# A batched two-stage attention with a squared-relu MLP: batch 0 cut by head sets and token parts, one PSUM tile with fixed banks, a new written order

## The chip, the cores and the metric

The kernel runs on one core of one Trainium2 chip. The metric is the device time of one execution in microseconds (us). Five engines work side by side, each in the order of its own instructions: PE (matrix products, with weight loads that overlap them), DVE and ACT (element-wise work; both can read PSUM, where PE puts its results), POOL and SP (here they issue DMA transfers, POOL the loads that turn float32 into bfloat16, SP the stores and the crossbar transposes).

## What is computed

```python
def _attn_ref(q, k, v, p):            # q, k, v: (8, 8, 576, 64); p: (8, 8, 32, 64)
    p_packed = sm_attn(p, k, v)       # softmax(p k^T / 8) v : 32 packed rows a head
    return sm_attn(q, p_packed, p_packed)

x = attn_out.transpose(0, 2, 1, 3).reshape(4608, 512)
h = x @ w_in                          # 512 x 2048
g = s * relu(h) ** 2 + b
out = g @ w_out                       # 2048 x 512
```

## The kernel before

**Stages.** Everything is done batch by batch (576 tokens each). A batch's q, k and v are loaded as 96 rows (`R`) by head by six tokens' columns; `Tk`/`Tq` (function `on_pe`) turn k and q on PE for batches 0 and 1, `Dk`/`Dq` (`on_dma`) by crossbar transposes from SP for batches 2 to 7. Heads are taken in two sets, a = 0 (even heads) and a = 1 (odd ones), and in four groups g. `F b.a` is the first attention's scores of one set and their exp; `P b` the packed rows and their division; `X b` turns them; `S b` is the second attention's scores and exp; `A b.a` the sums by a product with a block matrix of ones, then ln and exp(-x) on ACT and one multiplication on DVE, which gives the weights `aT`. The packed rows are multiplied into `w_in` first (`W b.ch`, chunks of 512 columns, result `pw`), so the first layer is `M b.m`: four products of 288 columns of `aT` with `pw`, 16 blocks m a batch, a relu on ACT (now and then DVE) and a square on DVE into `gT`. `O b.t x n` does n of the 16 products of one output tile; the last of them is followed by one scaling step on DVE (`ysb`) and by stores. The constant `b` comes in through `BT`/`BC`: sums of `w_out`'s columns by small products, then a float32 product with `rowsf` that adds four partial rows, into `biasrep`.

**Order.** A long written list of such words is run from top to bottom, and every instruction stays in that order on its engine (`keep_in_program_order`). A word issues its products and also the ACT and DVE steps that belong to them at that point. Loads stand in POOL's order, transposes and stores in SP's. What a word reads and what still occupies its buffer are its waits. `Z n` and `Y n` are n products of zeros of 512 columns, which only keep PE going; 12 more stand ahead of the list.

**Batch 0** differs: loads of k, q, v come in two halves by heads, its second scores and weights run by halves of the tokens (`weights_half`, `weigh_half`, `h 0.m.hf`), for two m blocks of the first layer in that form and for twelve in the usual one.

**Buffers.** PSUM has two pools: `psh` (two pairs of banks, for scores, W pairs, M) and `psy` (four single banks, for output tiles, packed rows, idle products). `rawp` has one buffer each for raw k, q and v; so the next load of k waits until its transposes have been read. `kT`, `qT` have two; `gT` holds three batches; `ysb` has five.

Of the kernel before, what the change touches and what calls it, by code (L numbers as in the profile page):

```python
# [14 lines left out]
def kernel(  # L15
# [32 lines left out]
    JJ = NP // 16  # L48

# [8 lines left out]
    psh = ctx.enter_context(tc.tile_pool(name="psh", bufs=2, space=bass.MemoryType.PSUM))  # L58
    psy = ctx.enter_context(tc.tile_pool(name="psy", bufs=4, space=bass.MemoryType.PSUM))
# [17 lines left out]
    early = []  # L77

    def big(dt=F32):
        if early:  # L80
            return early.pop()
        return psh.tile([P, 2, NB if dt == F32 else 2 * NB], dt, tag="h", name="hps")
# [12 lines left out]
    pn = [constp.tile([P, 2, 2, D], BF16, name=f"pn{i}") for i in range(2)]  # L95
    pall = constp.tile([16 * (B - 2), 16, 2, D], BF16, name="pall")
# [10 lines left out]
    rowsf = constp.tile([P, P], F32, name="rowsf")  # L107
# [7 lines left out]
    def load(what, b, h0=0, h1=H):  # L115
        src = {"k": k, "q": q, "v": v}[what]
        if h0 == 0:
            raw[what, b] = rawp.tile([R, H, NC * D], BF16, tag=what + "n", name=what + "n")
        pool.dma_start(
            out=raw[what, b][:, h0:h1, :],  # L120
            in_=src[b, h0:h1].rearrange("h (r c) d -> r h (c d)", c=NC),
        )

# [21 lines left out]
    def load_sb():  # L145
        sp.dma_start(out=svec[:], in_=moe_s[0:1].unsqueeze(0).to_broadcast([P, 1]))
        sp.dma_start(out=bvec[:], in_=moe_b[0:1].unsqueeze(0).to_broadcast([P, 1]))
# [6 lines left out]

    def prep_p(b):
        pt = big(BF16)
        for x in range(2):
            tr(
                pt[:, 0, x * P:(x + 1) * P],
                pn[b][:, x, :, :],  # L160
                identb[:],
            )
        for c2 in range(2):
            act.copy(
                out=pbd[D * c2:D * c2 + D, :, b, :, c2, :],
                in_=pt[D * c2:D * c2 + D, 0, 0:2 * P].rearrange("p (g a j) -> p a g j", g=4, a=2),
            )

    def prep_pall():
        n = 16 * (B - 2)  # L170
        pts = [psy.tile([P, 8 * P], BF16, tag="y", name="pps") for _ in range(2)]
# [6 lines left out]
        for x in range(2):  # L178
            src = pts[x][:].rearrange("p (t n) -> p t n", n=P)[:, :, 0:n].rearrange(
# [9 lines left out]
    def on_pe(b, what, half):  # L189
        dst = (kT if what == "k" else qT)[b % 2]  # L190
        if what == "q":
            dst = dst[:].rearrange("p h c r -> p (h c r)")
        tpw = big(BF16)
        tp = [tpw[:, 0], tpw[:, 1]]
        split = b == 0 and what == "q"
        if split:
            tp[1] = psy.tile([P, 2 * NB], BF16, tag="y", name="tps")
        for h4 in range(4):
            for cp in range(CP):
                o = (h4 % 2) * HS + cp * R  # L200
                tr(
                    tp[h4 // 2][:, o:o + R],
                    raw[what, b][:, 4 * half + h4, cp * P:(cp + 1) * P],
                    identb[0:R, 0:R],
                )
        d = dst[:, half * 4 * HS:(half + 1) * 4 * HS].rearrange("p (a s) -> p a s", a=2)
        if split:
            act.copy(out=d[:, 0], in_=tp[0][:, 0:2 * HS])
            vec.tensor_copy(out=d[:, 1], in_=tp[1][:, 0:2 * HS])
        else:  # L210
            vec.tensor_copy(out=d, in_=tpw[:, :, 0:2 * HS])
# [8 lines left out]
    def order_v(b, h0=0, h1=H):  # L220
        vec.tensor_copy(
            out=vr[:, :, h0:h1, 0:D].rearrange("r c h d -> r h c d"),
            in_=raw["v", b][:, h0:h1, :].rearrange("r h (c d) -> r h c d", c=NC),
        )

    def first_scores(b, a):
        if a == 0:
            e1[b] = attp.tile([R, 2, NC, 4, NP], BF16, tag="e1", name="e1")
        s1 = big()
        for g in range(4):  # L230
            for cp in range(CP):
# [8 lines left out]
                )  # L240
        act.activation(
# [8 lines left out]
    def packed(b, half=None):  # L250

        if not half:
            pps[b] = psy.tile([P, NB], F32, tag="y", name="pps")
        pp = pps[b][:, 0:2 * DV].rearrange("p (a x) -> p a x", a=2)
        for a in range(2):
            for c in range(NC):
                for g in range(4) if half is None else (2 * half, 2 * half + 1):
# [8 lines left out]
        if half == 0:  # L266
            return
        rd = smp.tile([P, 2], F32, tag="rd", name="rd")
        vec.reciprocal(out=rd[:], in_=pp[:, :, D])
        pk[b] = smp.tile([P, 2, 2, D], BF16, tag="pk", name="pk")  # L270
        for a in range(2):
# [6 lines left out]
    def turned(b):  # L278

        pt = pps[b][:, NB // 2:].bitcast(BF16)  # L280
        for a in range(2):
            tr(pt[:, a * P:(a + 1) * P], pk[b][:, a].rearrange("p c d -> p (c d)"), identb[:])
        vec.tensor_copy(
            out=ppd[b % 2][:].rearrange("p a g j -> p (a g j)"),
            in_=pt[:, 0:2 * P],
        )

    def second_scores(b, by_half=False, with_w=False):
        e2[b] = attp.tile([P, 2, S], BF16, tag="e2", name="e2")
        tiles = [big() for _ in range(2)]  # L290
        for a in range(2):
            for g in range(4):
                for c2 in range(2):
                    t, i = (c2, a) if by_half else (a, c2)
                    mm(
                        tiles[t][NP * g:NP * g + NP, i, 0:HS],
# [6 lines left out]
        if by_half:  # L303
            exp_half(b, tiles, 0, 0)
            exp_half(b, tiles, 1, 0)
            s2[b] = tiles
            return
        if with_w:
            packed_w(b, [0])
        for a in range(2):  # L310
            act.activation(
# [6 lines left out]
    def exp_half(b, tiles, a, hf):  # L318
        act.activation(
            out=e2[b][:, a, hf * HS:(hf + 1) * HS],  # L320
            in_=tiles[hf][:, a, 0:HS],
            func=AF.Exp,
            scale=scale,
        )

    def weights_half(b, hf):
        if hf == 0:
            aT[b] = atp.tile([P, 2, S], BF16, tag="aT", name="aT")
        dps = big()
        for a in range(2):  # L330
            mm(dps[:, a, 0:HS], onesbd[:], e2[b][:, a, hf * HS:(hf + 1) * HS], start=True, stop=True)
        if hf == 0:
            exp_half(b, s2[b], 0, 1)
            exp_half(b, s2[b], 1, 1)
        ld = smp.tile([P, 2, HS], F32, tag="ld", name="ld")
        act.activation(out=ld[:], in_=dps[:, :, 0:HS], func=AF.Ln)
        rcd[hf] = smp.tile([P, 2, HS], F32, tag="rcd", name="rcd")
        act.activation(out=rcd[hf][:], in_=ld[:], func=AF.Exp, scale=-1.0)

    def weigh_half(b, hf):  # L340
        cols = slice(hf * HS, (hf + 1) * HS)
        vec.tensor_tensor(out=aT[b][:, :, cols], in0=e2[b][:, :, cols], in1=rcd[hf][:], op=ALU.mult)

    def weights(b, a):
        if a == 0:
            aT[b] = atp.tile([P, 2, S], BF16, tag="aT", name="aT")
        dps = big()
        for hf in range(2):
            mm(dps[:, hf, 0:HS], onesbd[:], e2[b][:, a, hf * HS:(hf + 1) * HS], start=True, stop=True)
        ld = smp.tile([P, 2, HS], F32, tag="ld", name="ld")  # L350
        act.activation(out=ld[:], in_=dps[:, :, 0:HS], func=AF.Ln)
        rc = smp.tile([P, S], F32, tag="rcd", name="rcd")
        act.activation(out=rc[:], in_=ld[:].rearrange("p a s -> p (a s)"), func=AF.Exp, scale=-1.0)
        vec.tensor_tensor(out=aT[b][:, a, :], in0=e2[b][:, a, :], in1=rc[:], op=ALU.mult)

    def packed_w(b, chs):
        if b not in pw:
            pw[b] = atp.tile([P, 2, DFF], BF16, tag="pw", name="pw")
        where = {}
        if len(chs) > 1:  # L360
            pair = [big() for _ in range(2)]
            where = {(a, x): pair[a][:, x, :] for a in range(2) for x in range(2)}
        if len(chs) != 2:
            single = [psy.tile([P, NB], F32, tag="y", name="wps") for _ in range(2)]
            where.update({(a, len(chs) - 1): single[a][:] for a in range(2)})
        for x, ch in enumerate(chs):
            for g in range(4):
                for a in range(2):
                    mm(
                        where[a, x][NP * g:NP * g + NP],  # L370
                        ppd[b % 2][D * a:D * a + D, a, g, :],
                        w_in_sb[D * a:D * a + D, g, ch * NB:(ch + 1) * NB],
                        start=True,
                        stop=True,
                        tile_position=(D * a, NP * g),
                    )
        if len(chs) > 1:
            for a in range(2):
                dst = pw[b][:, a, chs[0] * NB:(chs[0] + 2) * NB].rearrange("p (i f) -> p i f", f=NB)
                evict(dst, pair[a][:], a == 0)  # L380
        if len(chs) != 2:
            ch = chs[-1]
            if b == 0 and ch == 0:
                s2["w"] = single
                first_w(b, 0)
                return
            for a in range(2):
                evict(pw[b][:, a, ch * NB:(ch + 1) * NB], single[a][:], a == 0)

    def first_w(b, half):  # L390

# [329 lines left out]
```

The softmax here doesn't subtract the row's maximum and nothing guards it: scores larger than these inputs give would overflow.

## Time and profile before

| What | us |
|---|---|
| three runs | 250.62, 251.31, 251.28 (median 251.28) |
| span of the profiled execution, first to last instruction | 248.0 |
| the same execution's total | not listed |
| PE busy / DVE busy / ACT busy | 241.6 / 144.4 / 140.6 |
| first product / end of the last product | 1.19 / 244.59 |

Stages by the timeline: batch 0's first layer starts at 20.37; batch 1's first scores at 36.69, batch 2's at 67.05; the second scores of batch 2 at 75.53. The last DVE step starts at 244.63 and the last store follows it.

```profile
DMA  6999999999696589939798999337998811121133
GB/s 74 174 206 208 201 203 204 197 204 162 136 213 140 140 138 144 225 89 193 115 209 169 160 147 226 85 80 156 146 230 133 185 37 50 42 46 42 42 87 86
```

These two rows of the page cut the span into 40 slices of 6.2 us: the busy share of the DMA engines in tenths, and the GB/s that they moved. In a table of groups, columns are line, engine, operation, output<-inputs, shape and count, then busy us and mean ns of one, then idle time just before and what ended it. Nearly everything has line L62, L65 or L73, since helpers record the instructions; one reads by the names of tiles. `hps` is a pair of banks of `psh`, `yps` an output tile, `zps` (and `hps<-zb`) the idle products.

### The profile page before, as it was taken

How to read it: one execution, taken by the hardware profiler on the slowest of the kernel's cores; microseconds unless marked ns; L12 is line 12 of the kernel's file. 1: busy time of each engine (PE TensorE's matmuls, PEld its weight loads, DVE VectorE, ACT ScalarE, POOL GpSimd, SP SyncE). 2: the span in 40 equal slices, each digit the busy share in tenths (PEclk: the TensorE clock that was granted, in tenths of full speed). 3: DMA queues.
4: the chain of work that ended last, by engine and by line, in shares of the span. 5: the costliest groups of instructions: out<-in, count | busy, mean ns of one | idle time of the engine just before them, and what ended most of it. 6: DMA issues, size and time to landing. Idle time of an engine off the chain costs nothing.

```text
span 248.0 us, 5518 instructions
## 1 busy us (share of the span) xinstructions
PE 241.6 (97%) x2302; PEld 134.2 (54%) x2302; DVE 144.4 (58%) x278; ACT 140.6 (57%) x218; POOL 29.1 (12%) x43
## 2 busy tenths in 40 slices
PE   8999899999999999999999999999999999999994
PEld 2655565356644665456544654466545654366453
DVE  4438875599564864386538753586348742767221
ACT  2266742558837772758555953888266844578000
POOL 8733212000300012000300030000200000000000
PEclk9999999999999999999999999999999999999999
DMA  6999999999696589939798999337998811121133
GB/s 74 174 206 208 201 203 204 197 204 162 136 213 140 140 138 144 225 89 193 115 209 169 160 147 226 85 80 156 146 230 133 185 37 50 42 46 42 42 87 86
DMA packets 59450, 35.50 MB, mean 143 GB/s; under 512 B 32160, under 2 KB 54944, under 8 KB 59424
## 3 DMA queue, kind: packets, MB, share of 16 engines
q0 software_dynamic: 25184, 18.61, 50.8%
q1 hardware_dynamic: 34192, 16.49, 30.2%
q8 instruction: 18, 0.29, 0.5%
q14 instruction: 8, 0.07, 0.1%
q10 hardware_dynamic: 48, 0.03, 0.0%
HBM read 37.23 MB, written 9.44 MB: 188 GB/s over the span
## 4 chain that ended last, share of the span: by engine, by line
PE 82%; DMA 16%; issue 1%; POOL 0%; DVE 0%; POOLq 0%
PE yps L62 49%; PE hps L62 31%; DMA w_out_sb<-in_moe_w_out_dram 14%; DMA kn<-in_k_dram 2%; PE pps L62 1%; PE pps L65 1%; POOL kn L73 0%; DVE ysb L73 0%; POOL identb L73 0%; POOLq L73 0%; POOLq L705 0%
## 5 line engine op out<-in xcount | busy, mean ns | idle before, releaser
L62 PE MATMUL yps<-w_out_sb,gT 128*128 128x512 bf16 (+1 forms) x592 | 147.8, 374 | 0.6 <-DMA w_out_sb<-in_moe_w_out_dram 0.6
L73 ACT ACTIVATE rlu<-hps 128x576 bf16<-128x576 f32 x124 | 77.0, 649 | 23.1 <-PE hps L62 19.9
L62 PEld LDWEIGHTS <-gT 128*128 128x128 bf16 x592 | 54.8, 98 | 50.9 <-issue 8.8
L62 PE MATMUL hps<-aT,pw 128*128 128x288 bf16 x512 | 78.3, 285 | 0.2 <-ACT rlu L73 0.2
L73 DVE TENSOR_TENSOR gT<-rlu 128x576 bf16<-128x576 bf16 x128 | 57.8, 457 | 26.1 <-ACT rlu L73 23.3
L62 PEld LDWEIGHTS <-pw 128*128 128x128 bf16 x512 | 49.7, 97 | 26.3 <-issue 1.2
L73 DVE SCALAR_TENSOR_TENSOR ysb<-yps,svec,biasrep 128x512 f32<-128x512 f32 (+1 forms) x37 | 27.0, 733 | 21.7 <-PE yps L62 21.5
L73 ACT ACTIVATE e<-hps 96x768 bf16<-96x768 f32 (+2 forms) x34 | 21.8, 693 | 30.8 <-PE hps L62 30.6
L73 ACT CAST pw<-hps 128x1024 bf16<-128x1024 f32 x14 | 14.2, 1012 | 21.6 <-PE hps L62 21.0
L73 DVE TENSOR_TENSOR aT<-e,rcd 128x576 bf16<-128x576 bf16 x16 | 12.1, 757 | 23.4 <-ACT rcd L73 23.2
L73 POOL DMA_DIRECT2D kn<-in_k_dram x9 | 6.9, 767 | 130.1 <-DMA kT<-kn 97.8
L73 DVE CAST pw<-hps 128x1024 bf16<-128x1024 f32 x14 | 17.1, 1220 | 4.7 <-PE hps L62 4.6
L62 PE MATMUL zps<-zb 128*128 128x512 bf16 x42 | 13.6, 452 | 1.2 <-DVE zb L73 1.2
L73 ACT ACTIVATE rcd<-ld 128x576 f32<-128x576 f32 x16 | 10.9, 683 | 0.5
L73 ACT ACTIVATE ld<-hps 128x576 f32<-128x576 f32 x16 | 10.3, 643 | 1.2 <-PE hps L62 0.4
L62 PEld LDWEIGHTS <-ppd 64*32 64x32 bf16 x384 | 3.8, 88 | 11.0 <-issue 8.1
L62 PEld LDWEIGHTS <-zb 128*128 128x128 bf16 x56 | 5.6, 108 | 7.2 <-issue 3.2
L73 DVE RECIPROCAL rd<-pps 128x2 f32<-128x2 f32 x8 | 1.4, 171 | 13.3 <-PE pps L62 13.3
L62 PE MATMUL hps<-w_in_sb,ppd 64*32 64x512 bf16 x224 | 8.9, 381 | 0.0
L62 PEld LDWEIGHTS <-kT 128*128 128x128 bf16 x192 | 6.9, 98 | 2.5 <-issue 0.5
L73 DVE COPY vr<-vn 96x3072 bf16<-96x3072 bf16 (+1 forms) x9 | 8.0, 893 | 0.1
L73 POOL DMA_DIRECT2D vn<-in_v_dram x9 | 6.7, 751 | 5.5 <-DVE vr L73 2.9
(58 smaller groups left out, 104.0 us busy)
## 6 DMA issues: line engine op xcount, KB each, us to landing
out_dram<-ysb SPq DMA_DIRECT2D x23, 192.0 KB, 2.6
kn<-in_k_dram POOLq DMA_DIRECT2D x7, 576.0 KB, 7.1
vn<-in_v_dram POOLq DMA_DIRECT2D x7, 576.0 KB, 10.7
qn<-in_q_dram POOLq DMA_DIRECT2D x7, 576.0 KB, 13.3
out_dram<-ysb SPq DMA_DIRECT2D x24, 128.0 KB, 2.4
w_in_sb<-in_moe_w_in_dram POOLq DMA_DIRECT2D x4, 512.0 KB, 14.3
w_out_sb<-in_moe_w_out_dram POOLq DMA_DIRECT2D x4, 512.0 KB, 18.7
out_dram<-ysb SPq DMA_DIRECT2D x23, 64.0 KB, 2.1
```

The lines of the kernel that those rows point to most:

```text
L62: return tc.keep_in_program_order(nc.tensor.matmul(*a, **kw))
L65: return tc.keep_in_program_order(nc.tensor.transpose(*a, **kw))
L73: return lambda *a, **kw: tc.keep_in_program_order(f(*a, **kw))
```

## The change

Batch 0 is cut anew. k and v come in two parts by head set (even heads, then odd), q in two parts by tokens (`PARTS`: four of each row's six tokens, then two); p comes from SP in float32 and DVE doubles and converts it. F, P, X and V of batch 0 run set by set; second scores (`S 0.u.a`), exp (`e`), sums (`d`), ln (`l`), exp(-x) (`i`) and multiplication (`G`) are words of their own for each part u and set a; its W runs in eight chunks of 256 columns, and its whole first layer in words `h 0.m.u` of two m blocks and one part.

The pools `psh` and `psy` are replaced by one tile of eight banks; each word names its banks (`@2`, `@6,2`). Functions become generators: a word's first mention issues its products, each later mention the next step on ACT or DVE, with a letter for the engine where there is a choice. An output tile's scaling and stores are the word `Q`. W of the other batches is issued chunk by chunk. The sum of the four partial bias rows moves from PE to DVE. `w_in` comes in parts in another order, with batch 1's k, v and q ahead of most of `w_out`; the scalars s and b come late, from POOL. The written order is new throughout; the idle products are 12 ahead of it and 26 in it, where there were 12 and 44.

```diff
+    PARTS = ((0, 2), (2, 3))
...
-    psh = ctx.enter_context(tc.tile_pool(name="psh", bufs=2, space=bass.MemoryType.PSUM))
-    psy = ctx.enter_context(tc.tile_pool(name="psy", bufs=4, space=bass.MemoryType.PSUM))
+    psp = ctx.enter_context(tc.tile_pool(name="psp", bufs=1, space=bass.MemoryType.PSUM))
...
+    banks = psp.tile([P, 8, NB], F32, name="banks")
+    spots = []
+
+    def take(n, dt=F32):
+
+        x = spots.pop(0)
+        t = banks[:, x:x + n, :]
+        return t if dt == F32 else t.bitcast(dt)
...
         pool.dma_start(
-            out=raw[what, b][:, h0:h1, :],
-            in_=src[b, h0:h1].rearrange("h (r c) d -> r h (c d)", c=NC),
-        )
+            out=raw[what, 0][:, 4 * part:4 * part + 4, :],
+            in_={"k": k, "v": v}[what][0].rearrange("(g a) (r c) d -> a r g (c d)", a=2, c=NC)[part],
+        )
+
+    def load_p0():
+        sp.dma_start(out=p0f[:], in_=p[0].rearrange("(x g) j d -> (g j) x d", x=2))
...
+    def scores0(u, a):
+        cols, w = part(u)
...
+        if u not in s2:
+            s2[u] = take(2)
+        qh = qT[0][:].rearrange("p h c r -> p h (c r)")
+        for g in range(4):
+            for c2 in range(2):
+                mm(
+                    s2[u][NP * g:NP * g + NP, c2, a * w:(a + 1) * w],
+                    ppd[0][D * c2:D * c2 + D, a, g, :],
+                    qh[D * c2:D * c2 + D, head(a, g), cols],
...
+    def inverse0(u, a):
+        act.activation(out=rcd["r", u][:, a], in_=rcd["l", u][:, a], func=AF.Exp, scale=-1.0)
...
-        ps = big()
-        mm(ps[:, 0, :], rowsf[:], biasrep[:], start=True, stop=True)
-        vec.tensor_scalar_mul(out=biasrep[:], in0=ps[:, 0, :], scalar1=bvec[:])
+        yield
+        vec.tensor_copy(out=bias4[:], in_=ps[0:NP, 0, :])
+        for g in range(1, 4):
+            vec.tensor_tensor(out=bias4[:], in0=bias4[:], in1=ps[NP * g:NP * g + NP, 0, :], op=ALU.add)
+        for g in range(4):
+            vec.tensor_scalar_mul(out=biasrep[NP * g:NP * g + NP], in0=bias4[:], scalar1=bvec[0:NP])
...
-        Lwi0 Lwi1 Lwo0 Lwi2 Lwi3 Lwo1 Lp1 Tk0.0 Z10 PD Tk0.1 Lk1 PP0 Z3 F0.0 V0.0 F0.1 Z5 P0.0 V0.1 Lv1
-        P0.1 Z1 Tq0.0 Z1 X0 Z1 Tq0.1 Lq1 Lwo2 Lwo3 Lpall Z3 S0 Z3 A0.0 Z1 W0.0 A0.1 G0.0 E Y8 h0.0.0
...
+        Lq0.1 Lp1 Lwi2.4 Z4@6 Tk0.0@2 Tk0.0a PD0 PP0@1 Lwi1.2 PP0v PP0a Z2@0 Tk0.1@4 Tk0.1v V0.0 Tk0.0a
+        Tk0.1a F0.0@6 F0.1@0 Lwi0.1 F0.0 Z2@3 P0.0@2 P0.0 Z3@6 X0.0 X0.0v F0.1 V0.1 Z3@0 P0.1 Z1@0
+        Tq0.0@4 Lk1 P0.1 X0.1 Z1@0 Tq0.1@3 Tq0.0a S0.0.0@6 X0.1a Tq0.0v S0.0.1 e0.1 Tq0.1v Z1@2 S0.1.0@0
+        Tq0.1a e0.0 Z2@2 S0.1.1 e1.0 d0.1@4 l0.1 d0.0 l0.0 Z1@6 W0.3@2 e1.1 i0.0 W0.3v PD1 W0.3v W0.2@6
+        d1.1@4 l1.1 i0.1 W0.2v W0.2a G0.0 i1.1 d1.0 l1.0 PP1@0 Lwi6.8 Lv1 G0.1 W0.1@2 W0.1v PP1a PP1v
+        Z2@1 h0.6.0@6 W0.1v i1.0 G1.0 h0.4.0@4 W0.0@0 h0.6.0a Lwi4.6 G1.1 h0.4.1@2 h0.6.0 h0.2.0@6
...
+        h0.10.1a Lpall Tq1.0v Tq1.1v h0.14.0 h0.8.0v h0.8.0 S1@6,2 S1 O0.1x2@4 PA O0.1x2 A1.0@6 S1
+        O0.0x1@5 A1.0 O0.3x1@0 h0.8.1 W1.3@2 W1.3a W1.3v O0.2x1@1 A1.1@6 A1.1 A1.1 O0.3x2 PPA0@2,3
...
+        O0.2x2 BT@2 O0.1x1 O0.0x1 Lk2 M1.0@6 M1.0a O0.1x1 PPA0 PPA0 O0.0x1 Lsb O0.3x1 Lv2 O0.3x1 M1.10
+        O0.1x1 O0.3x1 M1.6@6 O0.3x1 PPA0 BT O0.2x3 M1.6a M1.0 O0.0x1 M1.7@2 O0.0x2 Lq2 M1.7v M1.14@6
+        M1.14a V2 O0.0x2 M1.7 M1.6 M1.1@2 M1.1a M1.3@6 Dk2 O0.2x1 O0.0x2 O0.1x1 Lv3 O0.1x1 M1.9@2 M1.9a
+        O0.3x2 M1.1 O0.0x3 M1.3v M1.3 O0.2x1 F2.0@6 Dq2 O0.0x2 M1.9 PPA0 F2.0 Q0.3 M1.14 F2.1@2 F2.1
+        Q0.0 O0.2x2 M1.4@6 M1.4a P2.1@0 P2.1 M1.2@2 M1.15@6 X2 O0.1x2 M1.2a X2v M1.15a O0.1x1 Q0.1 M1.15
+        S2@2,6 S2 O1.0x1@0 S2 M1.4 M1.2 O0.2x2 M1.8@4 A2.0@2 A2.0 O0.2x2 A2.1@6 A2.1 M1.8v M1.8 O0.2x1
...
```

## The prediction

> **What bounds the kernel now.** I read the page first, then the groups of instructions by form, the busy times of three stretches, the timeline at the seams between stages, and last the landing times of the loads.
>
> ```profile
> span 248.0 us, 5518 instructions
> PE 241.6 (97%) x2302; PEld 134.2 (54%) x2302; DVE 144.4 (58%) x278; ACT 140.6 (57%) x218; POOL 29.1 (12%) x43
> PE 82%; DMA 16%; issue 1%; POOL 0%; DVE 0%; POOLq 0%
> ```
>
> ```profile
> L62 PE MATMUL zps<-zb 128*128 128x512 bf16 x42 | 13.6, 452 | 1.2 <-DVE zb L73 1.2
> L62 PE MATMUL hps<-zb 128*128 128x512 bf16 x14 | 3.7, 379 | 0.0
> L62 PE MATMUL hps<-biasrep,rowsf 128*128 128x512 f32 x2 | 1.1, 630 | 0.1
> ```
>
> ```profile
> 0.00:20.37 20.37, 18.92 (x200) 9.79 (x201) 9.76 (x30) 8.37 (x15) 12.04 (x21) 1.00 1.07 156
> 20.37:55.00 34.63, 33.11 (x356) 18.05 (x355) 25.43 (x47) 18.30 (x30) 5.58 (x7) 1.00 1.31 205
> 55.00:244.59 189.59, 189.59 (x1749) 106.37 (x1746) 108.74 (x203) 113.91 (x175) 11.47 (x15) 1.00 0.71 132
> ```
>
> ```profile
> 1.19 5.30 PE L62 MATMUL zps<-zb 128*128 128x512 bf16 x12 [1.19 <-DVE zb L73]
> 7.23 2.32 PE L62 MATMUL zps<-zb 128*128 128x512 bf16 x10
> 20.37 0.65 PE L62 MATMUL hps<-aT,pw 128*128 128x288 bf16 x4
> 60.05 0.65 PE L62 MATMUL hps<-aT,pw 128*128 128x288 bf16 x4
> 60.54 0.38 PE L62 MATMUL yps<-w_out_sb,gT 128*128 128x512 bf16 x1
> 72.13 1.47 PE L62 MATMUL yps<-w_out_sb,gT 128*128 128x512 bf16 x6
> 73.53 0.67 PE L62 MATMUL hps<-w_in_sb,ppd 64*32 64x512 bf16 x16
> 74.13 1.47 PE L62 MATMUL yps<-w_out_sb,gT 128*128 128x512 bf16 x6
> ```
>
> In the windows the columns are the stretch, then busy time (and count) of PE, weight load, DVE, ACT and POOL, clock, DMA share and GB/s. From 55 us to the last product PE has no gap at all. Its "97%" also counts 56 products of zeros, which do nothing. So the right question is how much of PE's time goes to products that are needed. I take starts, since durations overlap: an output product costs 0.2157 us (92 of them and the half ones run from 227.99 to 244.59), four first-layer products 0.49 (60.05 to 60.54). The same reading elsewhere gives 12 transposes 0.51, 12 first-score products 0.35, a chunk pair of W about 0.46, S 0.28, a sum pair A 0.245. A stretch on small array tiles costs extra at each edge: 72.13 to 73.53 is 1.40 where six products need 1.294, and the way back costs as much; start-to-start gaps give 93 and 95 ns. With these prices on the written order, the needed work is 223.6 us (70 edges among it, 6.6). The rest up to 244.59: start 1.19, idle products 14.6 (12 at 0.427 and 44 at 0.2157), waits 5.2. By 20.37, the first product of batch 0's first layer, only 4.9 us of needed work is done, so 15.5 us are lost there; 5.5 more are lost by 55 (8 idle products, 1.7, and 3.8 of waits).
>
> **What the Trainium skill says.** *TensorE: Matmul & The Clock Gate*, Part 1, has PE start at half clock until it has been busy for some 3.4 us; the trace agrees in size (0.427 against 0.216 us a product before and after about 7.2 us), though the clock column shows full speed. *TensorEngine Tiling (Array Packing)*, Key Properties, says a change of tiling mode drains the engine; the 93 and 95 ns are that price here. *DMA: Bandwidth & Descriptors*, Queues, rings and completion order, says each DMA engine goes round robin over its queues by packet, so a crossbar transpose beside a load slows both; the trace before never overlaps the two, so it cannot confirm this.
>
> **The change, part by part.** *Idle products.* 56 become 38: 12+4 at the head and 22 more. 18 at the warm price are 3.9 us of PE time; that is time only where something needed is ready instead.
>
> *Bias.* Two float32 products (0.93 us from 47.47 to 48.40) go. On DVE one 0.68 and one 0.75 become one copy, three adds from PSUM (as ysb, 0.75) and four multiplies (0.3 to 0.75; I take 0.4): 4.5 us, 3.0 more. DVE is then four us behind by my running sum, and M1.7 needs the bank those adds read; output products stand there on PE. Bounds 0 and 1.5; I take 0.5.
>
> *Batch 0's chain up to the first first-layer product.* k by head sets lands as now (5.86 and 8.23), p comes by SP earlier, off the path. The four extra idle products at the head end at 7.6 (two at half clock), so Tk0.0 starts then instead of at 6.29. ACT has four copies (0.64, 0.37, 0.64, 0.64, overlapping by about 0.06) to 10.1, and F0.0 reads 32 columns of the next heads, which lie in the other set, so both sets must be there: 10.3 (11.01 now). Exp 0.80, P0.0 at 11.75, its divisions, X0.0 at 12.95, then V0.1 on DVE (0.7), P0.1 at 14.25, Tq0.0 to 15.4, its 768-column copy on ACT (0.8) to 16.0, S0.0.1 at 16.45. The exps start at 16.75, as now (16.73): the head start is spent in the queues of ACT and DVE. ACT then holds eleven steps of 384 or 192 columns in a row (pitch about 0.43 and 0.26) until i0.1 ends at 20.6; G0.1 (0.55) ends at 21.3 and h0.6.0 starts at 21.35, one us later than now. But it has done more: W0.3, W0.2, W0.1 and PP1 are in, 5.96 us of needed work against 4.90. Nothing is won or lost here. Later arrivals of q by its 512 and 256 byte runs would add; bounds -1 and +1.
>
> *From there to the end.* Needed work is 223.6 - 0.9 - 5.96 = 216.75 (edges are again 70: W is split in four, but put beside other small-tile work). One more idle group of 4 is 0.86. PE so ends at 21.35 + 216.75 + 0.86 + W = 238.96 + W against 244.59, W being all waits after h0.6.0. The gain is 5.6 - W, so everything hangs on W (now 3.8 and 1.7 of idle products).
>
> W, first part: between h0.6.0 and S1 PE has 14.15 us of work, ACT 13.8 by its pitches, DVE 16.1. DVE starts 0.85 late (first product, relu), so it ends 2.8 behind; the last 1.6 us of it (h0.8.0 and h0.14.0) hold nobody up, and queue gaps cost about 0.8: 2.0, bounds 0.5 and 4. The loads in that stretch fit: the same bytes at the same rate put k1 at 22.7, w_in's rest at 25.2 and 30.6, q1 at 33.5, w_out from 36 to 44.4, each just ahead of its first use in the order.
>
> W, second part: batch 2's first stage is drawn forward, F2.0 from 67 to 54 and S2 from 75.5 to 58.9 plus earlier waits. It needs k2 and q2 loaded and turned.
>
> ```profile
> 40.89 0.77 POOL L73 DMA_DIRECT2D qn<-in_q_dram  x1 [1.36 <-PE pps L65]
> DMA to landing us min/median/max: 13.5/13.5/13.5
> L73 SPq DMA_TRANSPOSE qT<-qn x6: 2531/2840/3331, 56.3 to 189.2; - x6
> DMA to landing us min/median/max: 4.8/6.0/6.5
> ```
>
> q2 lands at 54.3 now, and the bytes ahead of it are the same. Its transpose takes 6.0 us: 60.5 at best, beside S2 at 58.9 + 2.5 = 61.4: no wait. At worst k2's transpose (from 48.7, beside the loads of v2 and q2) shares the engines fully: two back to back take 8.4 us (issued 56.30, landed 64.72), so one adds 4.2 and q2 lands at 58.5; then v3, queued as soon as V2 is done, adds its 2.9 to Dq2: 67.4, a wait of 6. Half of the 4.2 and none of the 2.9 gives 62.4, 1.0 late; between that and no wait I take 0.5. On SP the stores Q0.3 and on stand behind Dq2; five ysb buffers cover that.
>
> W, third part: from 60 us on ACT and DVE are never more than 2.9 us behind PE by the same sum, with three pairs of banks for first-layer products where there were two; 0.5 (0 to 2). Store order, Lsb on POOL, v0 by sets and the single pool with fixed banks cost nothing beside this: POOL is busy 12% of the span, and banks are waited for just as pool buffers were.
>
> W = 2.0 + 0.5 + 0.5 + 0.5 = 3.5. PE ends at 242.5. After it now come 3.4 us of store; Q7.1, a whole tile, now ends only 0.8 us before the last half tile, +0.2. Span 246.1. Around the span lie 251.28 - 248.0 = 3.3 us (the profiled execution's own total is not listed; I use the median of 250.62, 251.31, 251.28): **249.4 us**.
>
> **Rivals.** *B, hardly any wait (W = 1.3):* DVE's surplus hides behind squares nobody needs, and transposes overlap loads, as read and write side differ. For it: the uses stand just behind the landings. Against it: ACT, DVE and PE are all full at once. 247.2. *C, slower:* the transposes of batch 2 share the DMA engines with loads. PE is in order, so it stands at S2 although w_out and gT for dozens of output products are there. With q2 at 58.5 and half of v3's share, Dq2 lands at 66.0 and S2 starts at 66.2: W = 7.3 and 0.5 after it, 253.7 (255.1 with all of v3). It decides from a landing later than about 64.5, where W passes 5.6. For it: the skill's round robin, and DMA share above 1.2 until 54. Against: the transposes' packets are small and their landing is half issue time on SP (2.8 of 6.0). *D, it doesn't do what it says:* idle products go, and plain waits take their place; W = 5.6, 251.3.
>
> **How the numbers follow.** A (249.4) 0.47, its own range 248 to 250.8; B 0.17; C 0.24; D 0.12. A measurement here can tell 0.3%, 0.75 us. Faster: B, 0.43 of A, 0.01 of D = 0.61. Same: 0.03 of A, 0.09 of D = 0.12. Slower: C, 0.01 of A, 0.02 of D = 0.27. The range leaves out the outer half of C and a chain that begins a us sooner than B's: 246.3 to 254.4.
>
> **What would show it.** h0.6.0 at 21.35 within a us; exps of batch 0 from 16.75; PE's gaps between 25 and 40 ended by DVE; DVE behind after the bias adds; S2 near 62 with its gap, if any, ended by the q transpose; no gaps from 65 on; the last product at 242.5. I am wrong if the first h product comes near 18 (the chain, not W, was the gain), or if S2 waits past 64.5.

## The result, and the profile after

| | median, us | runs |
|---|---|---|
| before | 250.94 | 250.38 to 251.31, 6 runs |
| after | 253.59 | 252.34 to 259.12, 6 runs |

The ratio after/before is 1.0098, 95% interval 1.0070 to 1.0125: the change makes the kernel about 1% slower. The forecast was 249.4, faster. The number lies inside the stated range, but the sign is wrong. Runs more than 1.5% above the fastest of the same kernel (the 259.12 here, and some runs of e1, e2, e4 and e11) are left out of the ratios and of every median further down, where after's median is therefore 253.25.

The profiled execution of after took 253.94 us, of which its span is 252.1. Lines of its page, in the same parts as those shown of before:

```profile
span 252.1 us, 5616 instructions
PE 236.1 (94%) x2296; PEld 134.0 (53%) x2330; DVE 160.1 (63%) x324; ACT 126.3 (50%) x225; POOL 30.7 (12%) x45
PE 70%; DMA 18%; DVE 7%; issue 2%; ACT 1%; POOL 0%; POOLq 0%; DVEq 0%
PE banks L62 68%; DMA vn<-in_v_dram 11%; DMA kT<-kn 4%; DMA qT<-qn 3%; DVE vr L73 1%; PE banks L65 1%; DVE rlu L73 1%; DVE pw L73 1%; DVE pbd L73 1%; DVE aT L73 1%; DVE bias L73 1%; DVE gT L73 1%; DVE ysb L73 0%; ACT kT L73 0%; ACT e L73 0%
```

PE's share fell from 97% to 94% and its part of the chain that ended last from 82% to 70%. On that chain now stand two loads of raw v (v1 and v4), and the crossbar transposes of k and q. The chain before had 16% of DMA too, nearly all of it the load of `w_out` (14%) and one of k (2%), all of it before 43 us; raw v and the transposes did not stand in it. v1 costs little: its load lands at 29.27, DVE has been waiting 0.79 us for it and PE 0.62 for DVE:

```profile
29.29 0.96 DVE L73 COPY vr<-vn 96x3072 bf16<-96x3072 bf16 x1 [0.79 <-DMA vn<-in_v_dram]
30.30 0.56 PE L62 MATMUL banks<-vr,e 96*32 96x65 bf16 x48 [0.62 <-DVE vr L73]
```

So look at the body of the kernel, by stretches. After:

```profile
0.00:20.44 20.44, 16.43 (x217) 8.28 (x221) 8.85 (x31) 10.39 (x23) 12.94 (x22) 1.00 1.17 160
20.44:55.00 34.56, 32.55 (x388) 19.14 (x391) 31.40 (x67) 23.15 (x44) 6.79 (x10) 1.00 1.33 197
55.00:66.00 11.00, 8.28 (x112) 4.97 (x120) 4.89 (x12) 4.36 (x7) 0.87 (x2) 0.84 1.24 191
66.00:97.00 31.00, 30.48 (x216) 17.04 (x213) 21.44 (x41) 14.13 (x24) 3.19 (x5) 1.00 0.93 161
97.00:110.00 13.00, 11.77 (x167) 6.10 (x168) 8.44 (x15) 7.45 (x13) 0.74 (x1) 1.00 0.92 192
```

And two of the same stretches before:

```profile
55.00:66.00 11.00, 11.00 (x89) 7.58 (x87) 9.03 (x20) 9.77 (x18) 0.73 (x1) 1.00 0.92 164
97.00:110.00 13.00, 13.00 (x108) 5.86 (x108) 8.03 (x13) 6.71 (x10) 0.00 (x0) 1.00 0.85 160
```

Before, PE has no gap in either. After, it is idle for 2.7 us of 55 to 66, and DVE and ACT are half as busy as before there, so neither of them is what it waits for; the clock column reads 0.84. A second hole, 1.2 us, is in 97 to 110. (Small holes of 0.2 us with "issue" as their end are products whose records are missing: 562 of 592 output products are in the groups.)

**First hole.** PE's timeline (start, busy time, count, then idle time before and its releaser):

```profile
55.88 1.46 PE L62 MATMUL banks<-w_out_sb,gT 128*128 128x512 bf16 x6
59.80 0.82 PE L62 MATMUL banks<-pbd,kT 128*128 128x64 bf16 x12 [2.45 <-DMA kT<-kn]
60.43 1.04 PE L62 MATMUL banks<-w_out_sb,gT 128*128 128x512 bf16 x2
61.27 0.85 PE L62 MATMUL banks<-pbd,kT 128*128 128x64 bf16 x12
65.89 0.44 PE L62 MATMUL banks<-qT,ppd 64*32 64x288 bf16 x16
```

F2.0, batch 2's first scores, stands 2.45 us for the crossbar transpose of k2. Then the same work goes slower: two output products take from 60.43 to 61.27, 0.42 each where 0.2157 is usual, and twelve score products are busy for 0.82 instead of 0.52. The windows name it by the column after POOL, the clock:

```profile
57.00:60.00 3.00, 0.55 (x6) 0.21 (x5) 1.50 (x4) 0.00 (x0) 0.00 (x0) 0.96 1.07 118
60.00:63.00 3.00, 2.78 (x29) 1.81 (x27) 0.75 (x1) 1.61 (x2) 0.00 (x0) 0.50 1.28 153
63.00:66.00 3.00, 2.95 (x72) 1.91 (x79) 1.07 (x5) 1.84 (x3) 0.66 (x1) 0.97 1.04 284
```

So the stand costs twice: once as idle time, and once as 3.4 us at half clock. Cut where the clock column changes, the windows show how the two hang together:

```profile
56.33:59.74 3.41, 1.01 (x5) 0.28 (x3) 2.14 (x5) 0.41 (x1) 0.00 (x0) 1.00 1.37 123
59.74:63.16 3.42, 3.14 (x29) 2.17 (x31) 0.75 (x1) 1.61 (x2) 0.00 (x0) 0.50 1.28 162
```

The half clock fills one step of 3.41 us, and PE was busy for only 1.01 us of the step before. e4 below shows what else follows from such steps.

SP's queue and the answer for the tile `kT` show why k2 is late:

```profile
49.21 6.14 SPq L73 DMA_TRANSPOSE kT<-kn  x1
55.50 7.28 SPq L73 DMA_TRANSPOSE qT<-qn  x1
```

```profile
DMA to landing us min/median/max: 4.4/7.3/10.5
```

Its issue starts at 49.21 and it lands at 59.75: 10.5 us, the largest of the six. While it runs, the loads of v2 (landing 52.04), q2 (55.42) and v3 (issued 54.44, landing 62.90) move beside it, and from 55.50 on q2's transpose. The transpose of k3, with no load in flight, takes 4.4 us (75.76 to 80.14). q2's transpose, beside v3, takes 9.3.

**Second hole.** DVE and PE near 105 us, and the POOL issue that lies behind it:

```profile
104.41 0.96 DVE L73 COPY vr<-vn 96x3072 bf16<-96x3072 bf16 x1 [1.96 <-DMA vn<-in_v_dram]
105.29 1.28 DVE L73 CAST pw<-banks 128x512 bf16<-128x512 f32 x2
```

```profile
106.02 0.37 PE L62 MATMUL banks<-w_in_sb,ppd 64*32 64x512 bf16 x1 [0.69 <-DVE pw L73]
```

```profile
91.52 0.77 POOL L73 DMA_DIRECT2D qn<-in_q_dram  x1 [10.03 <-DMA qT<-qn]
92.28 0.77 POOL L73 DMA_DIRECT2D vn<-in_v_dram  x1
```

PE seems to wait for DVE (`pw`). But DVE, in order, had been standing 1.96 us in V4 (`vr<-vn`) for a load of v4 that landed at 104.39. That load was issued only at 92.28, since in POOL's order it stands behind the loads of k4 and q4, and q4's waited 10.03 us for the transpose of q3 to leave raw q. v4's own buffer had been free since V3 read it, from 75.9 on. The releaser at the end of a wait is not its cause; follow it back through the queues.

### The profile page after: what moved, and what is told of

The parts are those of the page before. It is cut to its first block, busy times and chain, and to the rows that moved or that the text cites. A ratio compares the mean times of both kernels' runs of the same rounds, so it can differ in the third digit from the quotient of the medians.

```text
span 252.1 us, 5616 instructions
## 1 busy us (share of the span) xinstructions
PE 236.1 (94%) x2296; PEld 134.0 (53%) x2330; DVE 160.1 (63%) x324; ACT 126.3 (50%) x225; POOL 30.7 (12%) x45
## 4 chain that ended last, share of the span: by engine, by line
PE 70%; DMA 18%; DVE 7%; issue 2%; ACT 1%; POOL 0%; POOLq 0%; DVEq 0%
PE banks L62 68%; DMA vn<-in_v_dram 11%; DMA kT<-kn 4%; DMA qT<-qn 3%; DVE vr L73 1%; PE banks L65 1%; DVE rlu L73 1%; DVE pw L73 1%; DVE pbd L73 1%; DVE aT L73 1%; DVE bias L73 1%; DVE gT L73 1%; DVE ysb L73 0%; ACT kT L73 0%; ACT e L73 0%
## 5 line engine op out<-in xcount | busy, mean ns | idle before, releaser
L62 PE MATMUL banks<-w_out_sb,gT 128*128 128x512 bf16 (+1 forms) x562 | 136.5, 375 | 2.4 <-issue 1.5
L73 ACT ACTIVATE rlu<-banks 128x576 bf16<-128x576 f32 (+2 forms) x100 | 59.2, 657 | 35.0 <-PE banks L62 30.4
L62 PE MATMUL banks<-aT,pw 128*128 128x288 bf16 (+2 forms) x512 | 74.1, 287 | 1.3 <-DVE rlu L73 0.8
L73 DVE TENSOR_TENSOR gT<-rlu 128x576 bf16<-128x576 bf16 (+2 forms) x128 | 55.6, 455 | 12.6 <-ACT rlu L73 8.6
L73 DVE SCALAR_TENSOR_TENSOR ysb<-banks,svec,biasrep 128x512 f32<-128x512 f32 (+1 forms) x37 | 26.8, 733 | 40.0 <-PE banks L62 32.7
L73 ACT ACTIVATE e<-banks 96x768 bf16<-96x768 f32 (+3 forms) x34 | 22.2, 694 | 46.3 <-PE banks L62 46.3
L73 DVE CAST pw<-banks 128x512 bf16<-128x512 f32 (+1 forms) x37 | 21.8, 612 | 8.6 <-PE banks L62 8.3
L73 DVE TENSOR_SCALAR rlu<-banks 128x576 bf16<-128x576 f32 (+2 forms) x28 | 21.0, 753 | 4.2 <-PE banks L62 3.4
L73 ACT CAST pw<-banks 128x512 bf16<-128x512 f32 (+1 forms) x35 | 17.2, 560 | 1.3 <-PE banks L62 1.0
L73 POOL DMA_DIRECT2D qn<-in_q_dram x9 | 7.0, 782 | 66.4 <-DMA qT<-qn 65.9
L73 DVE TENSOR_TENSOR aT<-e,rcd 128x576 bf16<-128x576 bf16 (+2 forms) x18 | 11.7, 684 | 0.4 <-ACT rcd L73 0.4
L73 ACT ACTIVATE ld<-banks 128x576 f32<-128x576 f32 (+2 forms) x18 | 10.2, 595 | 1.8 <-PE banks L62 1.1
```

The lines of the kernel that those rows point to most:

```text
L62: return tc.keep_in_program_order(nc.tensor.matmul(*a, **kw))
L73: return lambda *a, **kw: tc.keep_in_program_order(f(*a, **kw))
```

## The experiments

Each experiment starts from the changed kernel. In the diffs only the words of the written list that are touched are shown. W is here the end of the last product, less the start of h0.6.0, less the 217.6 us that the prediction's prices give for the needed work and one idle group; whatever an experiment adds is inside W. Milestones are starts on PE in the profiled execution, whose time is "profiled"; "ratio" is against before, with its interval.

| kernel | h0.6.0 | F2.0 | S2 | F4.0 | PE end | W | profiled | median | ratio |
|---|---|---|---|---|---|---|---|---|---|
| after | 20.4 | 59.8 | 65.9 | 126.2 | 248.2 | 10.2 | 253.94 | 253.25 | 1.0098 (1.0070 to 1.0125) |
| e1_warm | 20.6 | 59.9 | 64.4 | 133.4 | 256.7 | 18.5 | 262.40 | 251.56 | 1.0054 (1.0029 to 1.0079) |
| e2_v3_later | 19.7 | 58.2 | 62.7 | 132.6 | 254.7 | 17.4 | 260.42 | 256.43 | 1.0230 (1.0191 to 1.0269) |
| e3_v4_sooner | 20.0 | 59.8 | 65.8 | 124.7 | 246.8 | 9.2 | 252.53 | 252.61 | 1.0065 (1.0035 to 1.0094) |
| e4_no_k2_turn | 19.8 | 56.7 | 63.7 | 128.2 | 250.3 | 12.9 | 256.09 | 252.12 | 1.0040 (1.0020 to 1.0060) |
| e6_warm_v4 | 19.8 | 59.3 | 63.9 | 122.9 | 247.3 | 9.9 | 252.96 | 251.19 | 1.0030 (1.0017 to 1.0044) |
| e7_warm_v3_v4 | 19.7 | 58.5 | 63.0 | 121.9 | 244.0 | 6.7 | 249.73 | 249.92 | 0.9965 (0.9950 to 0.9979) |
| e8_all_bias_pe | 19.3 | 59.5 | 65.6 | 124.6 | 246.7 | 9.8 | 252.35 | 252.52 | 1.0069 (1.0043 to 1.0095) |
| e9_f2_later | 19.6 | 60.7 | 65.4 | 123.0 | 245.0 | 7.8 | 250.75 | 250.15 | 0.9986 (0.9974 to 0.9998) |
| e9b_f2_later_v3 | 19.3 | 59.9 | 65.2 | 122.8 | 244.9 | 8.0 | 250.62 | 250.36 | 0.9994 (0.9983 to 1.0006) |
| e10_v3_v4_order | 19.7 | 58.6 | 63.1 | 122.0 | 244.1 | 6.8 | 249.85 | 250.10 | 0.9979 (0.9967 to 0.9991) |
| e11_k2_on_pe | 19.6 | 58.1 | 62.6 | 121.7 | 243.7 | 6.5 | 249.53 | 249.53 | 0.9961 (0.9949 to 0.9973) |

Where the profiled time is far above the median (e1, e2, e4, and e6 by 1.8 us), the late stretches of the profile show how a load can come late, and F4.0, PE end and W are not those of the median. The start of h0.6.0 differs by up to 1.4 us although the list is the same up to there, so a milestone is best read with it.

### e1_warm: idle products in the stand

```diff
- O0.2x1 F2.0@6 Dq2
+ O0.2x1 Z11@6 F2.0@6 Dq2
```

> The changed kernel with eleven idle products (2.4 us) put just before F2.0, where PE stands 2.45 us for the transpose of k2. If the half clock that follows the stand costs time by itself: PE's clock stays at 1.00 from 57 to 66 us (0.50 between 60 and 63 now), F2.0 starts at 59.8 as now, S2 about 1.5 us earlier (64.9 for 65.9 if the q2 transpose ends it at 64.76), and the run is 0.5 to 1.5 us faster (252.1 to 253.1 against 253.6). If only the stand itself costs: same time within 0.3 us.

The windows of e1, and DVE near 109 us:

```profile
57.00:60.00 3.00, 2.98 (x17) 1.19 (x15) 1.70 (x4) 0.00 (x0) 0.00 (x0) 1.00 0.90 146
60.00:63.00 3.00, 3.00 (x84) 2.12 (x85) 1.00 (x3) 2.24 (x3) 0.00 (x0) 1.00 1.28 241
```

```profile
109.60 0.95 DVE L73 COPY vr<-vn 96x3072 bf16<-96x3072 bf16 x1 [8.59 <-DMA vn<-in_v_dram]
```

F2.0 starts where it did (59.9), as the transpose is as late as before. But the clock stays at 1.00 and PE does 84 products in 60 to 63 where after did 29; S2 comes 1.5 us sooner. So the half clock is an effect of the stand and costs about 1.5 us by itself. In this execution the saving is then lost many times over at v4, which lands at 109.58 and holds DVE for 8.59 us. The median, 251.56, is 1.7 us under after's, a little more than the 0.5 to 1.5 expected, though the intervals of the two ratios still overlap.

### e2_v3_later: v3 out of the way of q2's transpose

```diff
- O0.1x1 Lv3 O0.1x1 M1.9@2
+ O0.1x1 O0.1x1 M1.9@2
- W2.1@2 Lq3 W2.1v
+ W2.1@2 Lq3 Lv3 W2.1v
```

> The changed kernel with the load of v3 moved in POOL's order behind that of q3, so it starts only when q2 has been turned. Theory (transposes lose to loads in flight): the k2 transpose, 10.5 us from 49.2 now, is free of loads from 55.4 on instead of 62.9 and lands at 57 to 58.5, the q2 one 6 to 7 us after its issue at 55.5, at 62; F2.0 starts about 2 us sooner, 1.5 to 3 us off the total (250.6 to 252.1). Rival (a transpose beside stores and SP's own issue time sets it, not loads): both keep their 10.5 and 9.3 us and the time stays at 253.6.

At batch 2 it does what the theory says of q2: with no v3 beside it its transpose takes 5.2 us (54.69 to 59.94) instead of 9.3. k2's lands at 58.10 after 9.7, only 0.8 us shorter. F2.0 comes 1.6 us sooner, S2 3.2, of which 0.8 was there at h0.6.0. The total, however, is 3.2 us worse than after (median of three runs) where 1.5 to 3 better was expected. DVE in the profiled execution:

```profile
108.44 0.95 DVE L73 COPY vr<-vn 96x3072 bf16<-96x3072 bf16 x1 [9.20 <-DMA vn<-in_v_dram]
```

The transposed q3 comes later in this order (landing 93.19), the loads of q4 and v4 wait behind it, v4 lands at 108.42, and PE stands 7.9 us. That is one execution, 4.0 us above the median; but e10 below differs from e2 only by the place of v4 and takes 6.3 us less. A local gain is turned into a larger loss one batch later by the order of one queue.

### e3_v4_sooner: v4 ahead of k4

```diff
- O1.2x2 Lv4 M2.9v
+ O1.2x2 M2.9v
- M2.4@6 Lk4 M2.4a
+ M2.4@6 Lv4 Lk4 M2.4a
```

> The changed kernel with the load of v4 put ahead of that of k4 in POOL's order (it now stands behind k4 and q4, which wait for the transposes of k3 and q3, and lands at 104.39, with V4 holding DVE for 1.96 us before W3's evictions). Theory: the 1.7 us that PE loses between S3 and F4 go, 251.9. Rival (DVE is simply full there): DVE no longer waits in V4 but PE loses as much, 253.6.

v4 is issued at 76.07 and lands at 84.79. The time lost from S3 to F4.0 falls from 1.71 to 0.35 us, and W from 10.2 to 9.2; F2.0 and S2 stay. That is the price of v4's place by itself, 1.0 to 1.4 us. The medians point the same way (252.61 against 253.25; 251.9 was expected), but the intervals overlap. The rival, that DVE is simply full there, falls: PE no longer loses the time. There is a cost too: k3's transpose, now beside v4's load, takes 6.5 us for 4.4.

### e4_no_k2_turn: batch 2 without its k transpose

This kernel leaves out the transpose of k2; batch 2's first scores read the turned k of batch 0.

```diff
- M1.3@6 Dk2 O0.2x1
+ M1.3@6 O0.2x1
```

> The changed kernel without the transpose of k2: batch 2's first scores read batch 0's turned k, so that part of the result is left out, and nothing of that transpose runs or is waited for. Theory: the stand of 2.45 us at F2.0 and most of the 1.6 us behind it go, and q2 lands and turns sooner; 249.5 to 250.5. Rival (DVE and the banks set the pace there anyway, as the 1.3 us lost between S1 and F2.0 besides the stand suggest): PE stands for DVE instead, 252.5 or more.

F2.0 starts at 56.7, without a wait: the stand was k2's transpose and nothing else. PE then reaches S2 early, and stands there (first line); the windows below it are two steps of 3.41 us:

```profile
63.67 0.44 PE L62 MATMUL banks<-qT,ppd 64*32 64x288 bf16 x16 [2.37 <-DMA qT<-qn]
59.03:62.45 3.42, 2.27 (x61) 1.40 (x51) 2.18 (x7) 1.84 (x3) 0.00 (x0) 1.00 1.19 199
62.45:65.86 3.41, 2.19 (x27) 1.26 (x28) 1.21 (x4) 1.42 (x3) 1.43 (x2) 1.00 0.81 222
```

q2's transpose still takes 8.8 us (54.75 to 63.53), now with no other transpose ahead of it, only v3's load beside. So it is the load that stretches it.

This stand of 2.37 us, hardly shorter than after's 2.45, leaves the clock at 1.00. Its length is not what decides. In after, e1, e2, e3 and e4 the clock column falls once each inside the kernel, for 3.41, 6.83, 10.24, 3.41 and 3.41 us: whole multiples of one step. Counted back from the fall in such steps, PE was busy in the last one for 1.01 (after), 0.00 (e1), 0.12 (e2), 1.31 (e3) and 0.07 us (e4, which has a second stand of 3.58 us, for v4). No step with more was followed by a fall; the least is 1.43 us, in e1. The stand of 2.37 us lies across two steps of this count, and each keeps over 2 us of work.

The median, 252.12, misses the 249.5 to 250.5 expected: the wait moves to q2, and in the profiled execution v4 is late as well.

### e6_warm_v4 and e7_warm_v3_v4: the parts together

e6 is e1 with e3; e7 is e2 with e3 and six idle products (`Z6@6`) ahead of F2.0.

> Both edits at once: eleven idle products before F2.0 and v4 loaded ahead of k4. Theory (two waits for late transfers, each followed by PE at half clock, are what the change lost): S2 stays at some 3.8 us lost since h0.6.0 instead of 7.9, V4 waits for nothing, 4.5 to 5 us lost at the end instead of 10.2; 247.8 to 249, below the kernel before (250.6). Rival (DVE is too full, waits only move on): another wait takes their place and the run stays above 250.6.

> As the run before it, with v3 also behind q3 in POOL's order and six idle products before F2.0 for eleven. With v3 away the k2 transpose landed 1 us sooner (from its issue 9.7 for 10.5 us) and q2's took 5.2 for 9.3; if these set F2.0 and S2 in this version too, another 0.5 to 1.2 us go: 247 to 248.5. If v3 comes too late for batch 3 or pushes k3, the loss shows at F3 or S3.

e6 gains 2.1 us on after but misses its expectation by more than two. From e3 it differs only by the idle products, and it is 1.4 us faster: the price of the half clock once more. One part of its theory is empty: after v4's wait the clock stood at 1.00 in after too (97 to 110). In its profile, of the longest of its 22 runs, a further late load takes 1.7 us, that of v7; DVE, and PE behind it:

```profile
184.15 0.96 DVE L73 COPY vr<-vn 96x3072 bf16<-96x3072 bf16 x1 [3.79 <-DMA vn<-in_v_dram]
```

```profile
185.76 0.37 PE L62 MATMUL banks<-w_in_sb,ppd 64*32 64x512 bf16 x1 [1.65 <-DVE pw L73]
```

In e7 nothing comes late after F2.0: from S2 to the last product only 1.0 us is lost. v4's load and q2's transpose are in time, and the kernel is 3.3 us faster than after and 0.35% faster than before; the 247 to 248.5 expected it misses by 1.4. e2 alone lost 3.2 us; together with e3 it gains. The two edits can't be priced one by one.

### e8_all_bias_pe: the bias rows back on PE

e6 with the sum of the four partial rows of the bias as one float32 product, as before the change.

```diff
-        for g in range(1, 4):
-            vec.tensor_tensor(out=bias4[:], in0=bias4[:], in1=ps[NP * g:NP * g + NP, 0, :], op=ALU.add)
-        for g in range(4):
-            vec.tensor_scalar_mul(out=biasrep[NP * g:NP * g + NP], in0=bias4[:], scalar1=bvec[0:NP])
+        mm(ps[:, 0, :], rowsf[:], biasrep[:], start=True, stop=True)
+        vec.tensor_scalar_mul(out=biasrep[:], in0=ps[:, 0, :], scalar1=bvec[:])
```

> The version with eleven idle products and v4 ahead, and with the bias sums as they were (a float32 product on PE and two DVE steps instead of eight). If DVE's 3 us more cost PE what I put at 0.5 us (between S1 and F2.0), PE gains 0.5 to 1.3 there and gives 0.9 for the products, but F2.0 waits for k2 all the same and only stands longer: same as without this edit within 0.5 us. If DVE is what holds this stretch: 1 us faster.

252.52 against e6's 251.19: no gain, but 1.3 us of loss, where 0.5 either way or a gain of 1 was expected. PE's waits in this stretch are now

```profile
51.86 1.02 PE L62 MATMUL banks<-aT,pw 128*128 128x288 bf16 x7 [0.29 <-DVE biasrep L73]
65.61 0.44 PE L62 MATMUL banks<-qT,ppd 64*32 64x288 bf16 x16 [1.60 <-DMA qT<-qn]
```

The wait for DVE remains, and q2's transpose (10.7 us, beside a v3 on its way from 54.34 to 63.79) takes over at S2; why it is longer here than e6's 8.8 us is open. The rival that DVE's bias steps are what made the kernel slower falls.

### e9_f2_later and e9b_f2_later_v3: needed work ahead of F2.0

Three first-layer blocks of batch 1 and the output products among them go ahead of F2.0, three more blocks between F2 and S2; no idle products; v4 as in e3, and in e9b v3 as in e2. The first part of the edit:

```diff
- F2.0@6 Dq2 O0.0x2 M1.9 PPA0 F2.0 Q0.3 M1.14 F2.1@2 F2.1 Q0.0 O0.2x2 M1.4@6 M1.4a P2.1@0
+ Dq2 M1.4@6 O0.0x2 M1.9 PPA0 M1.4a Q0.3 M1.14 M1.2@2 Q0.0 M1.2a O0.2x2 M1.4 M1.15@6
+ M1.15a O0.1x2 M1.2 O0.1x1 M1.15 Q0.1 F2.0@2 F2.0 F2.1@6 F2.1 M1.8@4 M1.8v O0.2x2 P2.1@0
...
```

> Only PE's order around batch 2's first stage is changed: the output products and first-layer blocks that stood between F2.0 and S2, 3 us of them, come ahead of F2.0, four more blocks between F2.0 and S2; no idle products; v4 ahead of k4. Theory (drawing the stage forward exposed a transfer that was hidden): the stand of 2.45 us at F2.0 goes, the clock stays up, and 3 to 4 us fewer are lost at S2: 246.5 to 248.5, 1 us below the version with idle products. Rival (PE must stand somewhere until the q2 transpose at 64.8): the stand moves to S2 and the time is that of the idle products' version or worse.

> e9_f2_later (first-layer work of batch 1 ahead of F2.0, v4 ahead of k4) plus v3 behind q3, no idle products. Theory: with v3 out of the way q2's turn takes about 5.3 us instead of about 9, S2's wait goes, the wait before F2.0 stays at 0 to 1.3 us because v2 and q2 still run beside k2's turn; total 249.2 to 250.0 against 250.15 for e9. Rival (a further late load takes it back, as in e2): 251 or more, with a DVE step on v held over 2 us by a load.

e9 shows the theory from the other side: leave F2.0 later and the stand shrinks to 1.09 us (k2's transpose takes 11.9 here), the total to 250.15, 1.7 us above the 248.5 expected at most. e9b removes the stand, but not the time: its total stays within the interval of no change. In both, PE now waits in batch 2's W, from which words were moved away. PE in e9b:

```profile
68.81 0.85 PE L62 MATMUL banks<-w_in_sb,ppd 64*32 64x512 bf16 x9 [0.67 <-ACT rlu L73]
69.90 0.62 PE L62 MATMUL banks<-w_in_sb,ppd 64*32 64x512 bf16 x15 [0.24 <-DVE pw L73]
```

e9b was expected at 249.2 to 250.0; 250.36 misses that. No late load showed up (the rival), but these waits for steps on ACT and DVE did, and one of 0.55 us for DVE `ysb` at 61.33.

### e10_v3_v4_order: only the two loads moved

e2 with e3, no idle products.

> As e7_warm_v3_v4 (v3 behind q3, v4 ahead of k4) but without the six idle products, so that the stand before F2.0 is plain waiting. My theory: k2's turn still lands about 58.5 because its own loads v2 and q2 run beside it, so PE stands about 2 us before F2.0 and the clock column shows a dip in 57-66 (0.5 to 0.8); q2's turn takes about 5.3 us as in e7. The dip is then the only difference from e7's 249.92: total 251.0 to 252.0. Rival (idle products only fill a stand and the clock costs nothing): within 0.3 us of e7, 249.6 to 250.2.

Here my own theory was wrong in part. PE stands 1.69 us for k2's transpose:

```profile
58.59 0.52 PE L62 MATMUL banks<-pbd,kT 128*128 128x64 bf16 x12 [1.69 <-DMA kT<-kn]
58.95 0.60 PE L62 MATMUL banks<-w_out_sb,gT 128*128 128x512 bf16 x2
```

but the clock does not dip (0.60 for two output products, as usual), and the total is within 0.2 us of e7, as the rival had it. So the idle products of e7 are not what it gains by; the places of two loads are. From F2.0 to S2 the same words take 4.51 us here and 6.09 in after: 1.58 us is the measured price of the half clock.

### e11_k2_on_pe: k2 turned by PE

e10, with k2 turned as batch 1's k is.

```diff
- M1.3@6 Dk2 O0.2x1
+ M1.3@6 O0.2x1
- M1.3 O0.2x1 F2.0@6 Dq2 O0.0x2 M1.9 PPA0 F2.0
+ M1.3 Tk2.0@6 Tk2.0v O0.2x1 Tk2.0a Tk2.1@2 Tk2.1v Tk2.1a O0.0x2 F2.0@6 Dq2 M1.9 PPA0 F2.0
```

> As e10_v3_v4_order, but k2 is turned by 24 products on PE and four copies on DVE and ACT (as batch 1's k) instead of by the crossbar transpose. Cost on PE: two times 0.51 us. The 1.69 us stand before F2.0 should go, so F2.0 starts near 57.9 instead of 58.6 if the copies hold nobody up; lost time at the end 6.8 - 1.7 + 1.0 = 6.1; total 249.2 to 249.8 against 250.1. Rival (the stand only passes to the next late thing): q2's turn still lands at 60.4, S2 then comes near 62.4, so q2 should not take it over; but if it does, or if the copies add waits on the two pairs of banks, 250.0 or more and a gap before F2.0 or S2 named DVE kT, ACT kT or DMA qT.

```profile
56.43 0.68 PE L65 MATMUL banks<-identb,kn 96*128 96x96 bf16 x12
56.94 0.38 PE L62 MATMUL banks<-w_out_sb,gT 128*128 128x512 bf16 x1
57.16 0.67 PE L65 MATMUL banks<-identb,kn 96*128 96x96 bf16 x12
57.67 0.60 PE L62 MATMUL banks<-w_out_sb,gT 128*128 128x512 bf16 x2
58.10 1.07 PE L62 MATMUL banks<-pbd,kT 128*128 128x64 bf16 x24
```

The 1.02 us of products replaces 1.69 of standing, F2.0 starts at 58.1 with no gap, and q2's transpose, alone, takes 4.5 us. The median is 249.53 us, ratio 0.9961: the lowest of all, though its interval overlaps those of e7 and e10, 3.7 us under after and just measurably under before, by the expected amount.

## Why the prediction was wrong

**The sum.** Forecast: h0.6.0 at 21.35, W 3.5, tail 3.6, around the span 3.3. Measured: 20.44, 10.2, 3.9 and 1.8. So +6.7 (W) - 0.9 + 0.3 - 1.5 = +4.6, and to the rounding 249.4 became 253.94. W is a remainder and takes up any error in the price of the needed work: the trace names some 6.6 of its 10.2 us as PE's waits and slow clock (2.45 and 1.58 at F2.0, 0.9 each for `rlu` and for `pw`, 0.6 for `vr`, 0.2 for `aT`), the rest is starts that come later than the prices have them. The term around the span was mis-sized (I took it from the median of other executions than the profiled one) and hid 1.5 us of the error. That e11 ends at 249.53, next to the number forecast, is luck of the same kind: its W is 6.5 and not 3.5.

**The head** came 0.9 us sooner than forecast. F0.0 starts at 8.15 and not at 10.3, since its first products need only the first copies (it then waits 0.24 for DVE and 0.31 for ACT on the way), and the second exps start at 15.30, not 16.75. One us of the 2.2 at F0.0 came from PE's cold start: it ended at 5.3 us here, not at 7.2 as before, so the idle products were through and the first transpose began at 6.58 instead of 7.6. Part of that was given back at W0.3, which stood 1.16 us for a part of `w_in` that landed at 18.26. All twelve profiles after the change have h0.6.0 from 19.3 to 20.6, so the term was too high in each.

**W, term by term:**

| term | forecast | measured | read from |
|---|---|---|---|
| h0.6.0 to S1, DVE full | 2.0 | 2.3 | S1 starts at 36.91; DVE busy 14.94 of the 16.47 us, but PE's one long wait (0.62) is v1's load |
| bias steps on DVE | 0.5 | 0.6 | gap at 53.34, ended by DVE `rlu`; the steps take 4.75 us on DVE (forecast 4.5) |
| transposes of batch 2 | 0.5 | 4.2 | 2.62 from where F2.0 was due (57.18), 1.58 of half clock |
| rest up to S2 | 0 | 0.7 | what remains of 5.5 |
| from S2 on | 0.5 | 2.3 | 1.7 of it from S3 to F4.0, v4's load |

The step that failed is the one called "W, second part": "between that and no wait I take 0.5". The term measured 4.2. It asked only whether q2 would be there for S2. k2's transpose came into it as something that delays q2, never as something that F2.0 itself waits for. The paragraph has F2.0 at 54 plus 2.5 us of earlier waits, 56.5, and k2's transpose begin at 48.7: with the undisturbed 6.0 us that it used for q2, k2 is there at 54.7, in time; with the 10.5 us measured it is there at 59.75. So the overlap with loads was costed at nothing for k2, and for q2 at half of one transpose's share and none of v3.

What the runs showed in its place: a transpose beside loads takes about twice as long. For q2 they show it directly: 9.3 us beside v3 and 8.8 with k2's transpose gone but v3 there (e4), 5.2 with k2's transpose there but v3 gone (e2), 4.5 with neither (e11). For k2, v3 is 0.8 of the 10.5 us (9.7 in e2); that the loads of v2 and q2 make most of the rest no run took apart, but k3 goes the same way, 4.4 us alone in after and 10.0 beside the load of v4 in e6. q2 itself, at 64.76, did not hold S2 at 65.89. Two more things were not priced: that the stand would halve the clock (e1, e6 against e3, e10), and that loads queued behind transposes in POOL's order pass the delay on to a later batch ("W, third part", "0.5", with load order costed at nothing; e3).

**The rivals.** C had the right cause, transposes of batch 2 that share the DMA engines with loads, and 253.7 is next to the 253.59 measured; but it put the wait at S2, on q2. The place was F2.0, on k2 (S2 is where PE stands next, in e4 and e8), and the rest of the amount was the clock and v4. That the sums agree is partly chance. B's argument, that transposes and loads overlap freely, is refuted. The amount of DVE fullness (A's and D's worry) held to within 0.3 us. D's W of 5.6 makes 251.5 by the same sum as the others, not 251.3.

*DMA: Bandwidth & Descriptors*, Queues, rings and completion order, which the prediction drew on with no overlap in the trace to test it, has each DMA engine take its queues in turn, a packet at a time. The runs agree as far as the transposes go; what the loads lose they do not separate. *TensorE: Matmul & The Clock Gate*, Part 1, has PE fall back to half clock after an idle window of some 3.4 us, and has these windows run freely, whatever the kernel does. The step of 3.41 us in the clock column agrees. But the window need not be idle: 1.01 us of work in it (after) and 1.31 (e3) did not keep the clock up, 1.43 (e1) did. The measurement decides: a stand costs the clock if it leaves PE too little work in one such step, so by these figures one of about 2.1 us (3.41 - 1.31, an estimate) can be enough, and where it falls in the steps is chance.

**What stays open.** Why one run of a kernel has v4 in time and another not is not known; late loads were seen only in the profiled executions, one a kernel. Nor is the half clock in every run of after: one has a mean granted clock of 0.999, which leaves no room for such a step (it would take 0.007 off), and took 254.02 us all the same. e11 still loses 2.0 us between S1 and S2. The trace names three waits there, 0.85 us in all (0.21 for a part of `w_out`, 0.17 for DVE `aT`, 0.47 for DVE `rlu`); before has one, 0.57, for `w_out`. Removing them was not tried.

## What to carry to other kernels

When a change draws a stage forward, list every transfer that the stage reads with its earliest landing, and price it beside the loads that will then be in flight, not by its duration when alone. A load that waits for another buffer's transpose holds up all loads behind it in the same queue: put those whose buffers are free first. Edits to such an order must be tried together; two of them here lost 3.2 us and gained 0.6 singly, and gained about 3.1 as a pair.

## What the runs showed of the hardware

- A crossbar transpose of a 96x3072 bf16 tile took 4.3 to 6.6 us from issue to landing wherever no load of k, q or v moved beside it (4.4 to 6.5 in the kernel before), and 6.5 to 13.3 us where such loads moved beside it for six tenths of the time or more (13.3 is k6 in e6). Its issue on SP often grew with it, from 2.4 to 3.6 us in before to 6.1 for k2 and 9.7 for q3 in e2, but not always (2.5 for k4 in after, which took 7.3 to land).
- PE's clock fell to half for whole steps of 3.41 us, always after a step in which PE was busy for 1.31 us or less (1.39 at the end of e3), and never after one with 1.43 or more. One such step cost 1.58 us in after. A stand of 2.45 us in one step brought it, one of 2.37 across two steps did not. In this place the clock column shows it (0.50), while at the start of the kernel it shows full speed for products that take twice the usual time.
- Turning k2 by 24 products on PE cost 1.02 us of PE, less than the stand of 1.69 for the transfer that takes no PE time at all.
